# A sigmoid-attention and soft-MoE kernel: V products one unit behind their scores instead of two, two sigmoid buffers instead of three, 57 weight units loaded beside attention instead of 56

## The chip, the cores and the metric

One Trainium2 chip, one core of it. The metric is the device time of one execution in microseconds (us), as the median of several runs. Every engine has its own instruction queue, which it works through in order: PE (matmuls; PEld is its weight loads), DVE, ACT, POOL, and SP, which here only issues DMAs.

## The reference, cut to what matters

```python
# attention: batch 8, heads 12, sequence 448, head size 64, float32
scores = q @ k.T / sqrt(64) - log(448)
attn = 1 / (1 + exp(-scores))            # a sigmoid, no softmax
x = (attn @ v)                           # -> (8 * 448, 768)
# soft MoE: 8 experts, 4 slots each, inner size 1024
logits = x @ phi                         # (3584, 32)
d = softmax of logits over the 3584 rows
slots = d.T @ x                          # (32, 768)
slot_out[e] = relu(slots[e] @ w1[e]) @ w2[e]
out = (softmax of logits over the 32 slots) @ slot_out
```

## The kernel before, in words

**Attention.** The 96 heads go in 48 pairs (`NP`), of which one head lies on partitions 0 to 63 and the other on 64 to 127. Three units `(p, c)` with `c` 0 to 2 take 128 keys each of pair `p`, and a fourth, `c == NFK`, takes the last 64 keys of two pairs at once, so that two pairs make 7 units, a batch 21, and the whole 168 (list `seq`). A unit is: `score(u)`, four fp32 matmuls (eight passes on PE) of 64-by-64 weights and 448 columns, in the four quarters of the array, into a PSUM tile `sc` (L155 to L163); one sigmoid by ACT over 128 by 896 numbers into an SBUF tile `att` (L164, L165); `weigh(u)`, the four products of V with `att` into the PSUM tiles `av` (L168 to L190). There are two `sc` tiles and three `att` tiles.

**The order** is written by hand: one loop over steps `i` (L409) issues `score` of unit `i` and then `weigh` of unit `i - LAG`, with `LAG = 2`. All engines take their instructions in that order. The products of the last pair (three units) are issued at L177 on the whole height of the array, 128 by 64, instead of on quarters.

**Beside it.** When a pair's products are done, ACT copies one half out of PSUM (`evac_a`, L193) and DVE adds the other (`evac_b`, L197). DVE transposes x into `y` in small pieces (L212), so many us of them in a step as the table `rate` says (`PACE` where it says nothing). After each batch but the last, counted in steps from `u = (b + 1) * per_b + LAG`: `logits_job` in step u+1 (PE L230, DVE copies and maxima), `softmax_b` in step u+2 (two small sigmoids on ACT, L263 and L264), `softmax_c` in step u+3 (DVE L269 to L279), `slot_job` in step u+9 (PE L284, which needs all of `y` and what `softmax_c` made). The last batch is finished by `last_job`: logits (L230), softmax, slot inputs (L291, L295).

**The weights.** 128 units (64 of w1, 64 of w2) of 128 by 768 numbers, 384 KB each, pass through a ring of `N_A + N_B` = 70 SBUF tiles. `N_A` = 56 of them (`wa`) are there from the start and are filled beside attention, paced by L419. The other 14 (`wb`) lie in the memory that the attention tiles leave: their loads stand on SP behind the attention's loads (L465), in order, and each waits until the tiles that lay there were last used. The list `first` (L112) sets the order in memory: qk0, qk1, v0, vl, att0, qk2, x0, att1, att2, v1, x1, y. So the first `wb` tiles come free with the last scores, and the last three (`wb11` to `wb13`) only when `y` was last read, by the last slot matmuls (L291). From then on every load waits for a tile of the ring and goes out as w1 parts (L472), w2 steps (L579) and output tiles (L536, L537) free them; the output, 28 DMAs of 384 KB, ends the kernel.

Of the kernel before, what the change touches and what calls it, by code (L numbers as in the profile page):

```python
# [11 lines left out]
AF = mybir.ActivationFunctionType  # L12
# [5 lines left out]
DM, NSLOT, E, SPE, F = 768, 32, 8, 4, 1024  # L18
P = 128
NFK = 3  # L20
LAG = 2
PACE = 1.25
SLOT_AT = 9
W_STEPS = 140
# [2 lines left out]
NFC = F // P  # L27
HALF = DM // 2
UNIT = 768
N_A = 56  # L30
N_B = 14
QW = 2 * S
NP = B * NPR
WARM = 8
# [14 lines left out]
def soft_moe_attention(ctx: ExitStack, tc: tile.TileContext, qk, v, vl, phi, w1, w2, cst, out):  # L49
    nc = tc.nc  # L50
# [17 lines left out]
    def lt_of(b):  # L68
        return lts[b // 4][:, b % 4, :]
# [9 lines left out]
    def ring_tile(dt=F32):  # L79
        n = state["ring"]  # L80
        state["ring"] = n + 1
        n %= N_A + N_B
        if n < N_A:
            return wpa.tile([P, UNIT], dt, name=f"wa{n}")
        return state["wpb"].tile([P, UNIT], dt, name=f"wb{n - N_A}")

    def load_unit():
        n = state["next"]
        if n >= len(units):
            return  # L90
        state["next"] = n + 1
        u = units[n]
        t = ring_tile()[:]
        nc.sync.dma_start(t, w1[u[1:]] if u[0] == "w1" else w2[u[1:]])
        utile[u] = t
# [4 lines left out]
    with ExitStack() as actx:  # L100
# [8 lines left out]
        def hold(kind, n=""):  # L109
            return ap.tile(kinds[kind], F32, name=f"{kind}{n}")  # L110

        first = [("qk", 0), ("qk", 1), ("v", 0), ("vl", ""), ("att", 0), ("qk", 2), ("x", 0)]  # L112
        first += [("att", 1), ("att", 2), ("v", 1), ("x", 1)]
        held = {k: hold(*k) for k in first}
        xs = [held.pop(("x", t)) for t in range(2)]
        yt = ap.tile([P, 2, 4, TR, NBK, BLK], F32, name="y")
# [2 lines left out]
        def get(*k):  # L119
            return held.pop(k, None) or hold(*k)  # L120
# [16 lines left out]
        def load_qk(p):  # L137
            if p < NP:
                t = get("qk", p % 3)
                nc.sync.dma_start(t[:], qk[p])  # L140
                qkts[p] = t
# [13 lines left out]
        def score(u):  # L155
            p, c = u
            sc = ps_sc.tile([P, 2, 512], F32, name="sc")
            for t in range(2):
                pt, k0 = (p, c * P + t * 64) if c < NFK else (p + t, NFK * P)
                for h, r in enumerate(heads):  # L160
                    nc.tensor.matmul(  # L161
                        sc[64 * t:64 * t + 64, h, 0:S], qkts[pt][r, S + k0:S + k0 + 64], qkts[pt][r, 0:S],
                        start=True, stop=True)  # L163
            att = get("att", seq.index(u) % 3)  # L164
            nc.scalar.activation(att[:], sc[:, :, 0:S], AF.Sigmoid, bias=nbias[:], scale=QSCALE)  # L165
            atts[u] = att

# [40 lines left out]
        def turns(t, k0, n):  # L208
            def one(a, g):
                src = xs[t][32 * a:32 * a + 32, k0:k0 + n, :]  # L210
                src = bass.AP(src.tensor, src.offset + BLK * g, [src.ap[0], src.ap[1], [P, nblk(g)], [1, BLK]])
                nc.vector.transpose(ys[t][32 * g:32 * g + 32, a, k0:k0 + n, 0:nblk(g), :], src)  # L212

            for g in range(4):
                for a in range(4):
                    todo.append((0.0335 * n * nblk(g) + 0.18, lambda a=a, g=g: one(a, g)))
# [18 lines left out]
        def logits_job(b):  # L235
            lg = ps_sc.tile([P, 2, 512], F32, name="sc")[:, 0, :]
            logits(lg, b, range(NPR))
            nc.vector.tensor_copy(lt_of(b)[0:64, :], lg[0:64, 0:P])
            nc.vector.tensor_copy(lt_of(b)[64:128, 0:96], lg[64:128, 0:96])
            softmax_a(b)  # L240
# [16 lines left out]
            nc.vector.tensor_scalar(zt[:, 0:P], ls, new, None, op0=ALU.subtract)  # L257
            dts[b] = t1

        def softmax_b(b):  # L260
            zt, pe = dts[b][:, 0, :], dts[b][:, 1, :]
            n = P if b == 0 else P + 1
            nc.scalar.activation(pe[:, 0:n], zt[:, 0:n], AF.Sigmoid)  # L263
            nc.scalar.activation(zt[:, 0:n], zt[:, 0:n], AF.Sigmoid, scale=-1.0)  # L264

        def softmax_c(b):
            zt, pe = dts[b][:, 0, :], dts[b][:, 1, :]
            n = P if b == 0 else P + 1
            nc.vector.reciprocal(zt[:, 0:n], zt[:, 0:n])  # L269
            nc.vector.tensor_tensor(out=pe[:, 0:n], in0=pe[:, 0:n], in1=zt[:, 0:n], op=ALU.mult)  # L270
            nc.vector.transpose(zt[:, 0:P], pe[:, 0:P])
            if b == 0:
                nc.vector.tensor_reduce(out=mz[:, 2:3], in_=pe[:, 0:P], axis=AX.X, op=ALU.add)
            else:
                zb = small.tile([P, 1], F32, name="zb")
                nc.vector.tensor_reduce(out=zb[:], in_=pe[:, 0:P], axis=AX.X, op=ALU.add)
                nc.vector.scalar_tensor_tensor(
                    out=mz[:, 2:3], in0=mz[:, 2:3], scalar=pe[:, P:P + 1], in1=zb[:], op0=ALU.mult, op1=ALU.add)
            nc.vector.transpose(lt_of(b), lt_of(b))  # L279
# [19 lines left out]
        def slot_job(b):  # L299
            work(B * S)  # L300
            sl = ps_sc.tile([P, 2, 512], F32, name="sc")[:, 0, :]
            slot_mm(sl, dts[b][:, 0, 0:P])
            if b == 0:
                nc.vector.tensor_copy(acc[:], sl[:, 0:SLN])
            else:
                nc.vector.scalar_tensor_tensor(  # L306
                    out=acc[:], in0=acc[:], scalar=dts[b][:, 1, P:P + 1], in1=sl[:, 0:SLN],
                    op0=ALU.mult, op1=ALU.add)
# [71 lines left out]
        seq = []  # L380
# [4 lines left out]
        early, middle, late, rate = {}, {}, {}, {}  # L385
        for b in range(B):
            u = b * per_b + LAG
            late[u + 10] = [lambda: turns(0, 0, 3)]
# [3 lines left out]
        for b in range(B - 1):  # L392
            u = (b + 1) * per_b + LAG
            early[u + 1] = [lambda b=b: logits_job(b)]
            middle[u + 2] = [lambda b=b: softmax_b(b)]
            late[u + 3] = [lambda b=b: softmax_c(b)]
            late[u + SLOT_AT] = [lambda b=b: slot_job(b)]
            rate.update({u - 2: 1, u - 1: 1, u: 0, u + 1: 0, u + 2: 1.2, u + 3: 0.6, u + 4: 1.2})
        for i in range(u + 10, u + 31):
            rate[i] = PACE + 0.1  # L400
        todo = deque()
# [6 lines left out]

        for i in range(len(seq) + LAG):  # L409
            for f in early.get(i, ()):  # L410
                f()
            if i < len(seq):
                u = seq[i]
                score(u)
                if u[1] == NFK:
                    load_qk(u[0] + 3)
                elif u[0] % 2 == 1 and u[1] == NFK - 1:
                    load_qk(u[0] + 3)
                while state["next"] < min(N_A, (i + 1) * N_A // W_STEPS):  # L419
                    load_unit()  # L420
# [7 lines left out]
            for f in middle.get(i, ()):  # L428
                f()
            if i >= LAG:  # L430
                u = seq[i - LAG]
                weigh(u)
# [31 lines left out]

    for _ in range(N_B):  # L465
        load_unit()
# [184 lines left out]
```

## Time and profile before

| | before |
|---|---|
| median of 3 runs | 382.33 us (381.64 to 383.32) |
| the profiled execution, its own time | 382.41 us |
| its span, first instruction to last | 380.6 us |
| granted TensorE clock, mean of the span | 0.973 |
| PE busy | 357.8 us, 94% |
| ACT busy | 224.3 us, 59% |
| DVE busy | 252.7 us, 66% |
| DMA | 95.26 MB, mean 250 GB/s |

Read it by stages, not as one mean: until about 279 us PE works without a pause and the DMA queue has room; from about 285 us until the end the 16 DMA engines are busy without a pause, and PE waits now and then. Times in the views are us from the span's start. A matmul's end is modelled; a block of eight overlapping matmuls is listed with 0.93 us, though the next block starts 0.75 us after it.

### The profile page before, as it was taken

The page shows a single profiled execution, that of the slowest core. Times are in us where ns is not written, and L with a number is a line of the kernel's source. Part 1 is how long each engine was busy: PE and PEld are TensorE (multiplying, and loading weights), DVE is VectorE, ACT ScalarE, POOL GpSimd, SP SyncE. Part 2 cuts the span into 40 slices and gives each one's busy share as a digit, 9 for nine tenths or more (in the row PEclk, how much of TensorE's full clock was granted, in tenths as well). Part 3 has the DMA queues.
Part 4 walks back from the last instruction along what each step waited for, and adds up shares of the span by engine and source line. Part 5 has one row for each costly group of instructions (what it writes and reads, how often), then busy time and mean ns, then how long its engine had stood idle before and what let it go on. Part 6 is the DMA issues. An engine that isn't in the chain of part 4 may idle for free.

```text
span 380.6 us, 10176 instructions
## 1 busy us (share of the span) xinstructions
PE 357.8 (94%) x4132; PEld 158.4 (42%) x4132; DVE 252.7 (66%) x681; ACT 224.3 (59%) x310; POOL 4.9 (1%) x23
## 2 busy tenths in 40 slices
PE   8999999999999999999999999999999969989750
PEld 5444444444444444444444444444446533422430
DVE  0148868886889688788968896886846762132560
ACT  4777766766768677667767676776761213422450
POOL 0000000000000000000000000000000000100000
PEclk9999999999999999999999999999999987999895
DMA  7677575766656675757667575534369999999998
GB/s 258 212 252 255 165 257 176 254 217 189 219 190 216 235 241 197 236 180 246 213 186 250 169 236 203 146 102 134 91 219 388 397 397 400 397 400 395 396 399 301
DMA packets 42382, 95.26 MB, mean 250 GB/s; under 512 B 4448, under 2 KB 18528, under 8 KB 42336
## 3 DMA queue, kind: packets, MB, share of 16 engines
q1 hardware_dynamic: 42336, 94.62, 72.0%
q8 instruction: 32, 0.52, 0.5%
q14 instruction: 14, 0.11, 0.1%
HBM read 83.59 MB, written 11.01 MB: 249 GB/s over the span
## 4 chain that ended last, share of the span: by engine, by line
PE 83%; DVE 7%; DMA 3%; ACT 2%; issue 1%; DVEq 0%; ACTq 0%
PE sc L161 34%; PE av L190 33%; PE po L579 5%; PE sc L230 3%; PE sc L284 3%; DMA wb<-in_w_dram 2%; PE pt L517 2%; PE av L376 1%; PE ph L536 1%; DVE tmp L486 1%; DMA out_dram<-wa 1%; DVE tmp L485 1%; DVE wa L537 1%; PE pt L536 1%; PE av L177 1%
## 5 line engine op out<-in xcount | busy, mean ns | idle before, releaser
L165 ACT ACTIVATE att<-sc,nbias 128x896 f32<-128x896 f32 x168 | 169.2, 1008 | 85.2 <-PE sc L161 82.1
L161 PE MATMUL sc<-qk 64*64 64x448 f32 x1344 | 157.2, 538 | 0.4 <-ACT att L165 0.4
L212 DVE STREAM_TRANSPOSE y<-x 32x384 f32<-32x384 f32 (+5 forms) x352 | 143.4, 407 | 5.7
L190 PE MATMUL av<-att,v 64*64 64x448 f32 x1128 | 131.4, 536 | 0.0
L161 PEld LDWEIGHTS sc<-qk 64*64 64x64 f32 x1344 | 49.8, 133 | 72.6 <-issue 60.8
L190 PEld LDWEIGHTS av<-att,v 64*64 64x64 f32 x1128 | 43.1, 133 | 62.8 <-issue 61.3
L197 DVE TENSOR_TENSOR x<-x,av 128x448 f32<-128x448 f32 x47 | 29.2, 621 | 41.4 <-PE av L190 29.7
L579 PE MATMUL po<-wa,hw 128*32 128x384 f32 x224 | 24.8, 513 | 0.3 <-DMA wa<-in_w_dram 0.3
L193 ACT COPY x<-av 128x448 f32<-128x448 f32 x47 | 24.6, 523 | 0.0
L190 PE MATMUL av<-att,vl 64*64 64x448 f32 x192 | 22.4, 536 | 0.0
L472 PE MATMUL ph<-wa,phit 128*32 128x256 f32 x336 | 18.5, 379 | 0.0
L472 PEld LDWEIGHTS ph<-wa,phit 128*32 128x32 f32 x336 | 10.7, 110 | 6.9
L536 PE MATMUL ph<-lt,wb 128*128 128x384 f32 x28 | 12.7, 453 | 1.0 <-DVE lt L566 1.0
L537 DVE COPY wa<-pt 128x384 f32<-128x384 f32 x21 | 10.9, 554 | 2.9 <-PE pt L536 2.6
L537 ACT COPY wa<-ph 128x384 f32<-128x384 f32 x21 | 9.8, 480 | 4.9 <-PE ph L536 4.2
L230 PE MATMUL sc<-x,phit 128*32 128x96 f32 (+1 forms) x384 | 12.3, 262 | 0.3 <-DVE x L202 0.3
L230 PEld LDWEIGHTS sc<-x,phit 128*32 128x32 f32 x384 | 9.9, 110 | 6.2 <-ACT x L193 4.9
L536 PE MATMUL pt<-lt,wb 128*128 128x384 f32 x28 | 10.4, 373 | 1.6 <-DVE lt L566 1.6
L190 PEld LDWEIGHTS av<-att,vl 64*64 64x64 f32 x192 | 7.3, 133 | 10.7 <-issue 10.7
L306 DVE SCALAR_TENSOR_TENSOR acc<-acc,t,sc 128x192 f32<-128x192 f32 x6 | 2.5, 413 | 13.5 <-PE sc L284 13.5
L488 ACT COPY t<-tmp 128x32 f32<-128x32 f32 x8 | 1.7, 218 | 15.8 <-DVE tmp L486 15.8
L507 DVE CAST tmp<-lt 128x128 fp32r<-128x128 f32 x8 | 1.8, 227 | 13.7 <-PE pt L517 13.4
(106 smaller groups left out, 178.6 us busy)
## 6 DMA issues: line engine op xcount, KB each, us to landing
wa<-in_w_dram SPq DMA_DIRECT2D x112, 384.0 KB, 6.2
qk<-in_qk_dram SPq DMA_DIRECT2D x48, 448.0 KB, 3.5
v<-in_v_dram SPq DMA_DIRECT2D x48, 192.0 KB, 2.6
out_dram<-wa SPq DMA_DIRECT2D x21, 384.0 KB, 5.2
wb<-in_w_dram SPq DMA_DIRECT2D x16, 384.0 KB, 6.1
out_dram<-wb SPq DMA_DIRECT2D x7, 384.0 KB, 7.7
vl<-in_vl_dram SPq DMA_DIRECT2D x24, 64.0 KB, 2.6
csb<-in_cst_dram SPq DMA_DIRECT2D x1, 128.0 KB, 4.6
```

Of the source, the lines that this page charges most:

```text
L161: nc.tensor.matmul(sc[64 * t:64 * t + 64, h, 0:S], qkts[pt][r, S + k0:S + k0 + 64], qkts[pt][r, 0:S], start=True, stop=True)
L165: nc.scalar.activation(att[:], sc[:, :, 0:S], AF.Sigmoid, bias=nbias[:], scale=QSCALE)
L190: nc.tensor.matmul(o[t][r, 0:S], w, att[row, h, :], start=start, stop=stop)
L193: nc.scalar.copy(x_of(p), avs[p][1][:, 0:S])
L197: nc.vector.tensor_tensor(out=x_of(p), in0=x_of(p), in1=av[0][:, 0:S], op=ALU.add)
L212: nc.vector.transpose(ys[t][32 * g:32 * g + 32, a, k0:k0 + n, 0:nblk(g), :], src)
L230: nc.tensor.matmul(lg[32 * j:32 * j + 32, 0:BLK * nblk(j)], phi_sb[:, hp, :], blocks(x_of(b * NPR + hp), j, nblk(j)), start=(hp == 0), sto ...
L284: nc.tensor.matmul(sl[32 * a:32 * a + 32, 0:SLN], zt[:, c * BLK:(c + 1) * BLK], yt[:, :, a, :, c, :], start=(c == 0), stop=(c == NBK - 1))
L472: nc.tensor.matmul(ph[32 * j:32 * j + 32, 0:256], sT[:, kc, :], utile[("w1", e, j, kc // 3)][:, kc % 3 * 256:(kc % 3 + 1) * 256], start=(k ...
L536: nc.tensor.matmul(pf[:, 0:HALF], ct_of(m), st, start=True, stop=True)
L537: (nc.scalar.copy, nc.vector.tensor_copy)[n % 2](ov, pf[:, 0:HALF])
L579: nc.tensor.matmul(po[32 * fl:32 * fl + 32, 0:HALF], h[:, k:k + NSLOT], ut, start=(n == 0), stop=(n == 2 * E - 1))
```

## The change

`LAG` becomes 1: the order on PE is S(i), W(i-1), S(i+1), W(i) where it was S(i), W(i-2), S(i+1), W(i-1) (S for `score`, W for `weigh`). There are two `att` tiles instead of three, which leaves 3584 bytes of each partition; the ring gets 57 `wa` tiles and 13 `wb` tiles, and the list `first` another order. The two small sigmoids go to ACT one in step u+3 and one in step u+4 instead of both in step u+2, `softmax_c` to step u+5 instead of u+3, and the rates of the DVE transposes around them are shifted.

```diff
-LAG = 2
+LAG = 1
-N_A = 56
-N_B = 14
+N_A = 57
+N_B = 13
...
-        first = [("qk", 0), ("qk", 1), ("v", 0), ("vl", ""), ("att", 0), ("qk", 2), ("x", 0)]
-        first += [("att", 1), ("att", 2), ("v", 1), ("x", 1)]
+        first = [("qk", 0), ("qk", 1), ("v", 0), ("vl", ""), ("qk", 2), ("x", 0)]
+        first += [("att", 0), ("att", 1), ("v", 1), ("x", 1)]
...
-            att = get("att", seq.index(u) % 3)
+            att = get("att", seq.index(u) % 2)
...
-        def softmax_b(b):
+        def softmax_b(b, k):
...
-            nc.scalar.activation(pe[:, 0:n], zt[:, 0:n], AF.Sigmoid)
-            nc.scalar.activation(zt[:, 0:n], zt[:, 0:n], AF.Sigmoid, scale=-1.0)
+            if k == 0:
+                nc.scalar.activation(pe[:, 0:n], zt[:, 0:n], AF.Sigmoid)
+            else:
+                nc.scalar.activation(zt[:, 0:n], zt[:, 0:n], AF.Sigmoid, scale=-1.0)
...
-            middle[u + 2] = [lambda b=b: softmax_b(b)]
-            late[u + 3] = [lambda b=b: softmax_c(b)]
+            for k in range(2):
+                middle[u + 3 + k] = [lambda b=b, k=k: softmax_b(b, k)]
+            late[u + 5] = [lambda b=b: softmax_c(b)]
...
-            rate.update({u - 2: 1, u - 1: 1, u: 0, u + 1: 0, u + 2: 1.2, u + 3: 0.6, u + 4: 1.2})
+            rate.update({u - 2: 1, u - 1: 1, u: 0, u + 1: 0, u + 2: 1, u + 3: 1.2, u + 5: 0.6, u + 6: 1.2})
```

How that moves the instructions, at three places. The first is PE in the middle of attention, at the scores of unit 7 and what follows; the names in brackets are the semaphores for which a row waits (`Activation` counts ACT's instructions, `DMAHW` a landing). Before:

```order
L161 MATMUL sc_203<-qk2_90 64x448 [waits DMAHW7_49,Activation_49]
L161 MATMUL sc_203<-qk2_90 64x448 x3
L190 MATMUL av10_181<-att2_179,v1_94 64x448 x2
L190 MATMUL av11_182<-att2_179,v1_94 64x448 x2
L161 MATMUL sc_216<-qk2_90 64x448 [waits Activation_49]
L161 MATMUL sc_216<-qk2_90 64x448 x3
L190 MATMUL av10_181<-att0_195,v1_94 64x448 x2
L190 MATMUL av11_182<-att0_195,v1_94 64x448 x2
L161 MATMUL sc_231<-qk2_90 64x448 [waits Activation_49]
```

And the same scores now:

```order
L161 MATMUL sc_207<-qk2_89 64x448 [waits DMAHW7_49,PE_49]
L161 MATMUL sc_207<-qk2_89 64x448 x3
L190 MATMUL av10_174<-att0_199,v1_93 64x448 [waits Activation_49]
L190 MATMUL av10_174<-att0_199,v1_93 64x448
L190 MATMUL av11_175<-att0_199,v1_93 64x448 x2
L161 MATMUL sc_224<-qk2_89 64x448 [waits PE_49]
L161 MATMUL sc_224<-qk2_89 64x448 x3
L190 MATMUL av00_231<-att1_212,v0_162 64x448 [waits DMAHW2_49,DVE_49,Activation_49]
```

The wait for ACT has moved from the first matmul of a score (which needed the sigmoid of two units earlier, to have its `sc` tile back) to the first matmul of a product (which needs the sigmoid of its own unit); a score now waits only for PE's own matmuls of two units earlier.

The second place is PE at the end of attention: the last scores, the products of the last pair (L177, on another shape of the array), and the logits of the last batch (L230). Before:

```order
L161 MATMUL sc<-qk_3142 64x448 x4
L190 MATMUL av_3252<-att_3266,vl 64x448 x2
L190 MATMUL av_3293<-att_3266,vl 64x448 x2
L161 MATMUL sc<-qk_3142 64x448 x4
L177 MATMUL av_3293<-att_3278,v_3238 64x448 x2
L230 MATMUL sc<-x_91,phit 32x96 x2
...
L230 MATMUL sc<-x_95,phit 32x128 x2
L177 MATMUL av_3293<-att_3290,v_3238 64x448 x2
L177 MATMUL av_3293<-att_3304,v_3238 64x448 x2
```

And now:

```order
L161 MATMUL sc<-qk_3148 64x448 x4
L177 MATMUL av_3288<-att_3285,v_3233 64x448 x2
L161 MATMUL sc<-qk_3148 64x448 x4
L177 MATMUL av_3288<-att_3299,v_3233 64x448 x2
L230 MATMUL sc<-x_90,phit 32x96 x2
...
L230 MATMUL sc<-x_94,phit 32x128 x2
L177 MATMUL av_3288<-att_3308,v_3233 64x448 x2
```

The same matmuls stand there, but one product of the last pair now lies between the last two scores and one, not two, behind the logits: PE changes the shape five times instead of three.

The third place is SP behind attention, where the loads into the memory of the attention tiles stand. Before:

```order
L94 DMA wb2_3459<-in_w1_dram 128x768 [waits DMAHW7_49,DMAHW0_49,PE_49]
L94 DMA wb3_3461<-in_w1_dram 128x768 [waits PE_49,Activation_49]
L94 DMA wb4_3463<-in_w1_dram 128x768 [waits DMAHW6_49]
L94 DMA wb5_3465<-in_w1_dram 128x768 [waits DVE_49,PE_49]
L94 DMA wb6_3467<-in_w1_dram 128x768
L94 DMA wb7_3469<-in_w1_dram 128x768 [waits DMAHW1_49,PE_49,Activation_49]
L94 DMA wb8_3471<-in_w2_dram 128x768 [waits DMAHW2_49,PE_49,Activation_49]
L94 DMA wb9_3473<-in_w2_dram 128x768 [waits DMAHW3_49,DVE_49,PE_49]
L94 DMA wb10_3475<-in_w2_dram 128x768 [waits DMAHW4_49]
L94 DMA wb11_3477<-in_w2_dram 128x768 [waits DVE_49,PE_49,DMAHW5_49,Activation_49,Pool_49]
```

And now:

```order
L94 DMA wb2_3461<-in_w1_dram 128x768 [waits DMAHW1_49,DMAHW0_49,PE_49]
L94 DMA wb3_3463<-in_w1_dram 128x768 [waits DMAHW7_49,PE_49]
L94 DMA wb4_3465<-in_w1_dram 128x768 [waits DVE_49,PE_49]
L94 DMA wb5_3467<-in_w1_dram 128x768 [waits Activation_49]
L94 DMA wb6_3469<-in_w1_dram 128x768
L94 DMA wb7_3471<-in_w2_dram 128x768 [waits DMAHW2_49,PE_49,Activation_49]
L94 DMA wb8_3473<-in_w2_dram 128x768 [waits DMAHW3_49,DVE_49,PE_49]
L94 DMA wb9_3475<-in_w2_dram 128x768 [waits DMAHW4_49]
L94 DMA wb10_3477<-in_w2_dram 128x768 [waits DVE_49,PE_49,DMAHW5_49,Activation_49,Pool_49]
```

The row that waits for five semaphores, for the release of `y`, is `wb11` before and `wb10` now. Counted from 0 over all 128 units it is unit 67 both times (56 + 11 and 57 + 10). The wait for x0 (`DVE_49,PE_49`, released by the logits of the last batch) has come forward from `wb5` to `wb4`.

## The prediction

> **What bounds the kernel now.** I read the page, then the busy times by stage.
>
> ```profile
> span 380.6 us, 10176 instructions
> ...
> 4.83:279.25 274.42, 274.04 (x3229) 115.80 (x3229) 208.81 (x545) 191.61 (x229) 0.00 (x0) 1.00 0.63 203
> 279.25:287.34 8.09, 7.33 (x157) 5.32 (x159) 3.16 (x14) 4.28 (x12) 0.00 (x0) 1.00 0.92 310
> 287.34:352.68 65.34, 60.56 (x702) 26.41 (x691) 29.29 (x97) 17.13 (x47) 3.99 (x18) 0.95 1.03 396
> 352.68:380.60 27.92, 12.11 (x44) 7.36 (x44) 10.89 (x21) 9.78 (x21) 0.00 (x0) 0.75 0.96 365
> ```
>
> After the stage come its length and the busy times of PE, PEld, DVE, ACT and POOL; at the end the granted clock, the DMA share and GB/s. Attention (first row) is PE alone: 274.04 of 274.42 us, at full clock, DMA at 203 GB/s. From 287.34 us on the DMA engines are full, at 396 GB/s. So a change in attention counts if it moves PE, and behind attention only if it moves bytes or the moment from which they flow without a pause.
>
> Does anything make PE wait in attention? The groups:
>
> ```profile
> L165 ACT ACTIVATE att<-sc,nbias 128x896 f32<-128x896 f32 x168 | 169.2, 1008 | 85.2 <-PE sc L161 82.1
> L161 PE MATMUL sc<-qk 64*64 64x448 f32 x1344 | 157.2, 538 | 0.4 <-ACT att L165 0.4
> L161 PEld LDWEIGHTS sc<-qk 64*64 64x64 f32 x1344 | 49.8, 133 | 72.6 <-issue 60.8
> ```
>
> PE waited for a sigmoid 0.4 us in all, and a sigmoid takes 1.008 us. With the products two units behind, that is no wonder: between a score and its product PE has four other blocks of work (a product, a score, a product, a score). The change leaves two. So the question is how much of that cover a sigmoid uses, and I went to the timeline of a plain unit (start, length, engine):
>
> ```profile
> 139.88 0.93 PE L161 MATMUL sc<-qk 64*64 64x448 f32 x8
> ...
> 140.63 0.93 PE L190 MATMUL av<-att,v 64*64 64x448 f32 x8
> ...
> 140.94 1.01 ACT L165 ACTIVATE att<-sc,nbias 128x896 f32<-128x896 f32 x1 [0.50 <-PE sc L161]
> ...
> 141.39 0.93 PE L161 MATMUL sc<-qk 64*64 64x448 f32 x8
> ...
> 141.76 0.15 PEld L190 LDWEIGHTS av<-att,v 64*64 64x64 f32 x4 [0.22 <-issue]
> ...
> 142.14 0.56 PE L190 MATMUL av<-att,v 64*64 64x448 f32 x4
> ```
>
> A block starts every 0.75 us (139.88, 140.63, 141.39, 142.14), a unit takes 1.50. The score that starts at 139.88 has its sigmoid from 140.94 to 141.95. In the new order its product takes the block at 142.14. That is 0.19 us after the sigmoid's end, and the weights of that block, loaded at 141.76 now, can't be loaded so early, since the whole matmul, its weight load too, stands behind the wait.
>
> **The change part by part: the lag.** What does it cost PE when a sigmoid releases it? The trace shows it once, at the third score, which waits for the first sigmoid:
>
> ```profile
> 5.88 1.91 ACT L165 ACTIVATE att<-sc,nbias 128x896 f32<-128x896 f32 x2 [3.65 <-PE sc L161]
> 6.94 0.21 PEld L161 LDWEIGHTS sc<-qk 64*64 64x64 f32 x8 [1.15 <-ACT att L165]
> 6.94 0.98 PE L161 MATMUL sc<-qk 64*64 64x448 f32 x8 [0.38 <-ACT att L165]
> ...
> 7.74 0.93 PE L190 MATMUL av<-att,v 64*64 64x448 f32 x8
> ```
>
> The first of the two sigmoids ends at 5.88 + 1.008 = 6.89; the load starts at 6.94, so the release takes 0.05 us. The next block starts 0.80 us later instead of 0.75, so the weight load in the open costs 0.05. For the plain unit: 141.95 + 0.05 + 0.05 = 142.05, against 142.14. **Spare: 0.09 us; the wait costs nothing.** The other end: weight loads that stand in the open between blocks of different shape cost more, by the chain of waits:
>
> ```profile
> 144.57 1.45 PE sc L230 x42
> 146.02 0.91 PE sc L161 x8
> 147.68 0.75 PE sc L161 x8
> ```
>
> 0.91 - 0.75 = 0.16 us. With that, 141.95 + 0.05 + 0.16 = 142.16, which is 0.02 late. A score starts 0.75 us after the product before it, and that product hangs on the sigmoid of a score two places back, so one lateness is paid once in two units: 84 x 0.02 = 1.7 us. I take 0, because the row that shows this very wait is the nearer one; 1.7 is the upper end. A gain is excluded, since the blocks follow each other without a gap already.
>
> A load's own recorded duration is 133 ns (the third row of the groups). Even if all of it stood in the open, the product would start at 141.95 + 0.05 + 0.13 = 142.13, still in time.
>
> The longer lag had another use, to cover a late sigmoid. ACT's queue is late in one place of each batch:
>
> ```profile
> 148.56 1.01 ACT L165 ACTIVATE att<-sc,nbias 128x896 f32<-128x896 f32 x1 [0.47 <-PE sc L161]
> ...
> 149.47 0.30 ACT L263 ACTIVATE t<-t 128x129 f32<-128x129 f32 x1
> ...
> 149.80 0.32 ACT L264 ACTIVATE t<-t 128x129 f32<-128x129 f32 x1
> ...
> 150.02 0.52 ACT L193 COPY x<-av 128x448 f32<-128x448 f32 x1
> ...
> 150.43 2.08 ACT L165 ACTIVATE att<-sc,nbias 128x896 f32<-128x896 f32 x2
> ```
>
> Sigmoids follow each other by 1.50 us, so the next was due at 148.56 + 1.50 = 150.06, and started at 150.43, 0.37 late, behind two small sigmoids and a copy. With the new lag this would have cost 0.37 - 0.09 = 0.28 us, seven times: 2.0 us. That is what the split prevents. A small sigmoid starts 0.91 us after a big one and holds ACT for 0.33 (149.47 to 149.80): 148.56 + 0.91 + 0.33 = 149.80, before 150.06. Steps u+3 and u+4 have no copy (the third and seventh unit of seven bring one). A copy alone fits too: 0.91 + 0.53 = 1.44, under 1.50. The small sigmoid's input is ready in step u+2 already, where it runs now. Nothing late is left on ACT, so this costs and brings 0.
>
> `softmax_c` on DVE starts two units later. Its reader is the slot job; DVE's pieces that must precede that end earlier:
>
> ```profile
> 157.50 1.47 DVE L212 STREAM_TRANSPOSE y<-x 32x96 f32<-32x96 f32 x5
> ...
> 159.64 1.51 PE L284 MATMUL sc<-y,t 128*32 128x192 f32 x32
> ```
>
> 158.97 against 159.64, 0.67 us spare. DVE does the same work without a hole in another order, and transposes fill the time until the second small sigmoid: 0. If that cover went, a hole of up to 2 x 1.50 = 3.0 us less 0.67 would be paid at each slot job.
>
> SP's V loads hang on the products, which come one block earlier against the scores; they land in 2.6 us (the page's part 6) and are used four units, 6 us, later. The 57th weight load is 0.39 MB in 274 us at 203 of 396 GB/s: no cost. Beginning of the kernel: the third score or the first product waits for the same sigmoid, 0.
>
> **The end of attention** has two more changes of array shape.
>
> ```profile
> 277.49 0.93 PE L161 MATMUL sc<-qk 64*64 64x448 f32 x8
> ...
> 278.35 0.97 PE L177 MATMUL av<-att,v 128*64 128x448 f32 x4
> ```
>
> 278.35 - 277.49 - 0.75 = 0.11 for one, and 0.16 for the score after logits above: 0.27, so **+0.3 us** on everything that waits for the last product.
>
> **The 57th unit.** Behind attention DMA is the limit, so a unit loaded earlier is worth 393,216 bytes / 396 GB/s = 0.99 us, if the queue doesn't run dry. It could: the loads stand in order and unit 67 waits for `y` in both kernels, with 11 `wb` loads ahead of it before and 10 now. The waits of SP's queue between 268 and 289 us, the issues at its release, and the landings (us, minimum, median, maximum) of the first two `wb` loads and of the last three:
>
> ```profile
> SPq L94 <- PE av L291: 2.0, 1, 2.0
> ...
> 287.54 1.28 SPq L94 DMA_DIRECT2D wb<-in_w_dram  x3
> ...
> L94 SPq DMA_DIRECT2D wb<-in_w_dram x2: 328/379/430, 272.1 to 273.9; - x2
> ...
> DMA to landing us min/median/max: 3.0/3.1/3.2
> ...
> L94 SPq DMA_DIRECT2D wb<-in_w_dram x3: 328/423/430, 287.5 to 288.4; - x3
> ...
> DMA to landing us min/median/max: 5.0/5.6/6.1
> ```
>
> With an empty queue a load lands in 3.0 us; unit 67 took 5.0, so 2.0 us of work stood ahead of it. One unit less leaves 1.0: the queue doesn't run dry, and the full 0.99 counts. Against it stands the 0.3 us above, and that `wb4` to `wb7` are released later than their neighbours (for x0 the logits, now behind one more product). The 1.0 us left would hide the 0.3; since I can't show that the late releases leave it whole, I charge the 0.3.
>
> Sum: 382.4 (profiled execution; median 382.33) - 0.99 + 0.3 + 0 = **381.7 us**.
>
> **The rivals.** *No gain from the 57th unit*: the later release of x0 eats the last 1.0 us of queue, and the gate of unit 67 sets the end in both: 382.4, with the end of attention 382.7. For it: the gate has not moved. Against: 2.0 us of queue.
>
> *Slower, products with an open weight load*: the weights of a product whose wait ended late are not loaded under the score that is still streaming but behind it. Then each product pays the 0.05 us of the third score, 165 x 0.05 = 8.3, that is 390.7 us (at 0.16 even 26 us). It decides as soon as a sigmoid ends after the point of early load, which is 141.76 in the plain unit, and it ends at 141.95 there. For it: no row shows a late release while PE is streaming. Against: the loads at 141.76 run under a score that uses the same rows of the array and cost its block nothing.
>
> A rule of the Trainium skill would make this rival the forecast. "TensorE: Matmul & The Clock Gate", section "The mechanism" (packing of small matmuls), says that weight loads overlap running matmuls only where their row groups differ; by it the time would be 390.7 us, by the row at 141.76 it is 381.7. The row differs from the rule, and I go by the row.
>
> *Faster*: between 279 and 285 us DMA is not full.
>
> ```profile
> 279.00:285.00 6.00, 5.72 (x76) 3.64 (x74) 1.59 (x8) 3.50 (x9) 0.00 (x0) 1.00 0.86 274
> ```
>
> At 396 GB/s 6 x (1 - 274/396) = 1.85 us could be had there. If the releases that come earlier (the products of unit 164, which free `wb2`, end one block sooner) fill it, this comes on top of 0.99 less 0.3: 382.4 - 0.7 - 1.85 = 379.9. Against: most of the releases there have not moved forward.
>
> **How the numbers follow.** Forecast 0.60, no gain 0.20, slower 0.13, faster 0.07. A measurement of this kernel tells about 0.5%, 1.9 us, from no change: forecast and no gain lie within it (0.80), the others outside. The three runs spread from 381.64 to 383.32, 0.7 below and 1.0 above their median. Forecast less 0.7 is 381.0, no gain plus 1.0 is 383.7. The lower end goes 0.5 further, for a hole between 279 and 285 us that is filled in part. So 380.5 to 383.7 holds the forecast and no gain, 0.80, and the 1.7 us of the wait's upper bound (381.7 + 1.7 = 383.4).
>
> **What would show it.** Right: a plain unit still takes 1.50 us, with the product's weight load about 0.05 us behind its sigmoid's end and not 0.38 ahead of the block; the slot jobs start when they did; unit 67 lands about 4 us after its issue; attention ends 0.3 us later and the span 0.7 us earlier. Wrong: units of 1.55 us, big sigmoids that start late behind something else on ACT, a slot job that waits for DVE, or a DMA share under 1 between 287 and 291 us.

## The result, and the profile after

| | before | after |
|---|---|---|
| median | 382.39 us (381.22 to 383.44, 20 runs) | 383.47 us (381.89 to 385.47, 20 runs) |
| the profiled execution, its own time | 382.41 us | 383.62 us |
| its span | 380.6 us | 381.8 us |

The changed kernel takes 1.0029 of the time before, 95% interval 1.0018 to 1.0040: 0.7 to 1.5 us slower. A second comparison, on another chip (e13 below), gave 1.0017 (1.0002 to 1.0031), and both hold a loss of 0.7 to 1.2 us. The time lies inside the range of the forecast only because the range was drawn wide enough for the rival without a gain; the direction was wrong: 0.7 us less was forecast, and about 1 us more came.

Attention first. The groups of the profile after (busy time and mean of one, then the idle time before them and what ended it):

```profile
L165 ACT ACTIVATE att<-sc,nbias 128x896 f32<-128x896 f32 x168 | 169.1, 1007 | 86.8 <-PE sc L161 84.3
L161 PE MATMUL sc<-qk 64*64 64x448 f32 x1344 | 157.2, 539 | 0.0
L190 PE MATMUL av<-att,v 64*64 64x448 f32 x1128 | 131.4, 536 | 0.4 <-ACT att L165 0.4
L190 PEld LDWEIGHTS av<-att,v 64*64 64x64 f32 x1128 | 41.2, 131 | 65.4 <-ACT att L165 61.5
```

The weight loads (PEld) of the products now wait for sigmoids, 61.5 us in all, but the products themselves only 0.4 us, at the first one. Two plain units in the timeline after:

```profile
132.81 1.01 ACT L165 ACTIVATE att<-sc,nbias 128x896 f32<-128x896 f32 x1
...
133.26 0.93 PE L161 MATMUL sc<-qk 64*64 64x448 f32 x8
...
133.87 0.29 PEld L190 LDWEIGHTS av<-att,v 64*64 64x64 f32 x8 [0.46 <-ACT att L165]
134.01 0.93 PE L190 MATMUL av<-att,v 64*64 64x448 f32 x8
...
134.76 0.93 PE L161 MATMUL sc<-qk 64*64 64x448 f32 x8
...
135.51 0.93 PE L190 MATMUL av<-att,v 64*64 64x448 f32 x8
```

The sigmoid ends at 132.81 + 1.01 = 133.82, the load starts at 133.87, the block at 134.01, and the next product 1.50 us later. The wait is there and costs nothing.

The end of attention in the timeline after, then in that before:

```profile
276.99 0.93 PE L161 MATMUL sc<-qk 64*64 64x448 f32 x8
277.85 0.97 PE L177 MATMUL av<-att,v 128*64 128x448 f32 x4
278.76 0.98 PE L161 MATMUL sc<-qk 64*64 64x448 f32 x8
279.67 0.97 PE L177 MATMUL av<-att,v 128*64 128x448 f32 x4
280.57 1.30 PE L230 MATMUL sc<-x,phit 128*32 128x96 f32 x40
281.80 0.97 PE L177 MATMUL av<-att,v 128*64 128x448 f32 x4
282.70 0.55 PE L221 MATMUL av<-csb,x 128*128 128x128 f32 x3
```

```profile
275.98 0.93 PE L161 MATMUL sc<-qk 64*64 64x448 f32 x8
276.73 0.93 PE L190 MATMUL av<-att,vl 64*64 64x448 f32 x8
...
280.48 1.72 PE L177 MATMUL av<-att,v 128*64 128x448 f32 x8
282.13 0.66 PE L221 MATMUL av<-csb,x 128*128 128x128 f32 x4
```

The first transposes of x (L221) start at 282.70 instead of 282.13, 0.57 us later: 0.31 from the shape changes (from the last score but one to the first transposes 5.71 us, before 6.15 with one block of 0.75 us more in between), 0.19 from six slot products, each of which holds PE for 1.47 us now (before 1.44), and 0.08 from the start.

Then the DMA engines. Busy times by stage (the last two columns are the DMA share and GB/s), before and after:

```profile
276.00:284.00 8.00, 7.72 (x97) 3.60 (x90) 2.58 (x9) 5.57 (x10) 0.00 (x0) 1.00 0.62 201
284.00:288.00 4.00, 3.52 (x106) 3.07 (x108) 2.78 (x15) 1.40 (x6) 0.40 (x2) 1.00 1.00 369
288.00:292.00 4.00, 4.00 (x74) 2.36 (x70) 2.71 (x13) 0.31 (x1) 0.21 (x1) 1.00 1.04 389
292.00:300.00 8.00, 8.00 (x156) 4.79 (x151) 6.39 (x24) 1.58 (x6) 0.42 (x2) 1.00 1.02 391
```

```profile
276.00:284.00 8.00, 7.72 (x97) 2.97 (x89) 1.70 (x6) 5.95 (x10) 0.00 (x0) 1.00 0.67 191
284.00:288.00 4.00, 3.52 (x102) 3.33 (x102) 2.77 (x13) 1.54 (x7) 0.00 (x0) 1.00 1.02 374
288.00:292.00 4.00, 4.00 (x75) 2.31 (x70) 2.59 (x13) 0.31 (x1) 0.61 (x2) 1.00 0.98 334
292.00:300.00 8.00, 8.00 (x152) 4.81 (x148) 6.39 (x24) 1.58 (x6) 0.42 (x2) 1.00 1.00 383
```

The queue is full from 288 us on before (1.04, 389 GB/s); after, it isn't (0.98, 334). In a second profile of the changed kernel (e13 below) the rate of this stage is 371 GB/s, between the two, at a share of 1.07: the rate tells more than the share. From 276 to 300 us the changed kernel moves 8 x 10 - 4 x 5 + 4 x 55 + 8 x 8 = 344 KB less, 0.87 us at 396 GB/s. That is nearly the whole 57th unit (393 KB), which had come before 276 us.

### The profile page after: what moved, and what is told of

Read it like the earlier page. It is cut to its first block, busy times and chain, and to the rows that moved or that the text cites. A ratio compares the mean times of both kernels' runs of the same rounds, so it can differ in the third digit from the quotient of the medians.

```text
span 381.8 us, 10246 instructions
## 1 busy us (share of the span) xinstructions
PE 358.0 (94%) x4132; PEld 155.9 (41%) x4132; DVE 253.9 (66%) x681; ACT 223.7 (59%) x310; POOL 4.9 (1%) x23
## 4 chain that ended last, share of the span: by engine, by line
PE 76%; DMA 11%; DVE 6%; ACT 2%; issue 1%; DVEq 0%; SPq 0%; ACTq 0%
PE sc L161 34%; PE av L190 33%; DMA wa<-in_w_dram 8%; PE sc L230 3%; PE sc L286 3%; DMA wb<-in_w_dram 2%; PE av L378 1%; DMA out_dram<-wa 1%; DVE tmp L489 1%; DVE tmp L488 1%; PE av L177 1%; ACT lt L500 1%; DVE lt L499 1%; DVE cz L502 1%; DVE lt L505 1%
## 5 line engine op out<-in xcount | busy, mean ns | idle before, releaser
L190 PEld LDWEIGHTS av<-att,v 64*64 64x64 f32 x1128 | 41.2, 131 | 65.4 <-ACT att L165 61.5
L582 PE MATMUL po<-wa,hw 128*32 128x384 f32 x228 | 27.9, 494 | 0.4 <-DMA wa<-in_w_dram 0.3
L475 PE MATMUL ph<-wa,phit 128*32 128x256 f32 x342 | 19.8, 379 | 0.0
L539 PE MATMUL ph<-lt,wb 128*128 128x384 f32 x28 | 11.8, 421 | 1.1 <-DVE lt L569 1.0
L230 PE MATMUL sc<-x,phit 128*32 128x96 f32 (+1 forms) x384 | 12.3, 262 | 0.3 <-DVE x L202 0.3
L230 PEld LDWEIGHTS sc<-x,phit 128*32 128x32 f32 x384 | 9.9, 110 | 6.2 <-PE sc L161 4.9
L582 PEld LDWEIGHTS po<-wa,hw 128*32 128x32 f32 x228 | 6.6, 108 | 12.9 <-DMA wa<-in_w_dram 5.5
L539 PE MATMUL pt<-lt,wb 128*128 128x384 f32 x28 | 9.5, 341 | 1.6 <-DVE lt L569 1.6
L286 PE MATMUL sc<-y,t 128*32 128x192 f32 x224 | 10.7, 329 | 0.0
```

The lines of the kernel that those rows point to most:

```text
L190: nc.tensor.matmul(o[t][r, 0:S], w, att[row, h, :], start=start, stop=stop)
L230: nc.tensor.matmul(lg[32 * j:32 * j + 32, 0:BLK * nblk(j)], phi_sb[:, hp, :], blocks(x_of(b * NPR + hp), j, nblk(j)), start=(hp == 0), sto ...
L286: nc.tensor.matmul(sl[32 * a:32 * a + 32, 0:SLN], zt[:, c * BLK:(c + 1) * BLK], yt[:, :, a, :, c, :], start=(c == 0), stop=(c == NBK - 1))
L475: nc.tensor.matmul(ph[32 * j:32 * j + 32, 0:256], sT[:, kc, :], utile[("w1", e, j, kc // 3)][:, kc % 3 * 256:(kc % 3 + 1) * 256], start=(k ...
L539: nc.tensor.matmul(pf[:, 0:HALF], ct_of(m), st, start=True, stop=True)
L582: nc.tensor.matmul(po[32 * fl:32 * fl + 32, 0:HALF], h[:, k:k + NSLOT], ut, start=(n == 0), stop=(n == 2 * E - 1))
```

## The experiments

Two theories at first. One puts the loss into attention: the lag of one makes it longer, and the buffers that it leaves come late. The other puts it behind attention, into the 57th unit and the order of the buffers.

**e1_lag1_56**: the changed kernel with the ring of before.

```diff
-N_A = 57
-N_B = 13
+N_A = 56
+N_B = 14
```

> The changed kernel with 56 units beside attention and 14 behind it, as before; lag, sigmoid buffers and split stay changed. Theory A (the late end): attention ends 0.57 us later (in the trace of the changed kernel the first transposes on PE start at 282.70 us instead of 282.13), this alone makes the loss and the 57th unit brings nothing or a little: 383.4 to 384.2 us, at or above the changed kernel. Theory B (the short queue): the loss comes from the 57th unit, which leaves fewer loads queued when unit 67 is released, so that the DMA engines run short between 289 and 294 us; with 14 loads behind attention the queue covers the late end again: 382.3 to 382.7 us, as before the change.

Measured: 1.0032 (1.0017 to 1.0047), as the first theory has it. It is no clean test: with two sigmoid buffers the memory lies differently, and it is unit 66, not 67, that waits for `y`.

**e2_lag2_57**: the changed kernel with the old lag; 57 units, two buffers and the split stay.

```diff
-LAG = 1
+LAG = 2
```

> The changed kernel with the products two units behind their scores, as before; two sigmoid buffers, split and 57 units stay. Each sigmoid then waits for the product two units back to release its buffer, which ends 0.13 us after the sigmoid could have started by the trace's plain unit; no wait on PE expected, attention ends where it ended before (282.1 us) give or take 0.2. Theory A: no loss, and the 57th unit's 0.99 us in part: 381.5 to 382.4 us. Theory B: the queue is short here too: 382.9 to 383.5 us.

Measured: 0.9996 (0.9977 to 1.0015). Without the lag there is no loss. The 57th unit with its full 0.99 us should have given 0.9974, just outside this interval; with what the split costs (told below) the kernel gained 0.2 us.

**e3_old_tail**: the changed kernel with the last two products issued together, so three shape changes as before.

```diff
-            if i >= LAG:
+            if i >= LAG and i != len(seq) - 2:
                 u = seq[i - LAG]
+                if i == len(seq) - 1:
+                    weigh(seq[i - LAG - 1])
```

> The changed kernel with the products of the last pair put together again, three changes of array shape at the end instead of five (the last two scores stand together). Attention ends about 0.3 us earlier than in the changed kernel. Theory A: 383.2 us, 0.3 less than the changed kernel's 383.5. Theory B: within 0.2 us of the changed kernel, since the queue is as short.

Measured: 1.0025 (1.0007 to 1.0043). With the old tail there is still a loss; the 0.3 us of the tail itself are too small to be read from this interval.

**e4_before_late**: the kernel before with 0.55 us of extra matmuls ahead of the last transposes.

```diff
+                        warm(pw, 2)
                         turn_pe(px[0], p - 1)
```

> The kernel before with two idle matmuls (four passes, about 0.55 us by the ones already there: six passes take 0.83 us) put on PE behind the last product, so that attention ends as late as in the changed kernel, with 56 units. Theory A: slower by 0.5 to 1.1 us: 382.9 to 383.5 us. Theory B: the 2.0 us of loads that stand ahead of unit 67 hide it: 382.3 to 382.6 us.

Measured: 0.9995 (0.9980 to 1.0010), as the second theory has it. But in its trace the first load that waits for `y` goes out only 0.43 us later (287.97 us), 0.14 us when a start that was 0.29 us slower is set aside: other work hid most of the delay. It doesn't show that a late release is free.

**e5_att_new** and **e6_att_old**: attention alone, of the changed kernel and of that before; everything from the weight ring's second part on is left out and the slot inputs are written out instead.

```diff
+    nc.sync.dma_start(out[0:P, 0:NKC * NSLOT].rearrange("p (k s) -> p k s", k=NKC), sT[:])
```

> Attention of the changed kernel by itself: everything behind the last slot inputs is left out (no loads behind attention, no experts, no combination; one small DMA of the slot inputs ends it). Read beside the same cut of the kernel before. Theory A (the lag costs in attention itself, more than one profile shows): 0.8 to 1.3 us more than the cut of the kernel before. Theory B (what the traces show is all: 0.3 us for two more changes of array shape, 0.03 us at each of six slot jobs): 0.4 to 0.6 us more, and the rest of the 1.1 us loss arises behind attention.

> Attention of the kernel before by itself, cut at the same place (no loads behind attention, no experts, no combination). About 288 us by the trace of the kernel before, where the last slot inputs are there at 287.9 us, with some 4 us for the DMA and the end: 290 to 293 us. It is the measure for the cut of the changed kernel.

Measured: 293.88 us (292.74 to 293.93) and 292.77 us (292.24 to 293.25), in ratios to the whole kernel 0.7663 (0.7650 to 0.7676) and 0.7642 (0.7630 to 0.7654). So attention is 0.8 to 1.1 us longer. The two profiled executions lie 1.6 us apart: 0.48 us arise between the eleventh score and the first transposes, with the block by which the lag moves that score set aside (the tail and the slot products again), 1.1 us at the start. The start is told in the last section; it varies from run to run in both kernels, so 0.5 us is what the change itself costs in attention.

**e7_unsplit**: the changed kernel with both small sigmoids in step u+2, as before.

```diff
-            for k in range(2):
-                middle[u + 3 + k] = [lambda b=b, k=k: softmax_b(b, k)]
-            late[u + 5] = [lambda b=b: softmax_c(b)]
+            middle[u + 2] = [lambda b=b: [softmax_b(b, k) for k in range(2)]]
+            late[u + 3] = [lambda b=b: softmax_c(b)]
```

> The changed kernel with both small sigmoids, the softmax behind them and the transposes' rates where they were before the change (step u+2, u+3), so that the split alone is undone. By the working of the prediction a big sigmoid then starts 0.37 us late once a batch, the product one unit behind waits 0.28 us for it, seven times 2.0 us: about 2.0 us more than the changed kernel, 385.4 us. The rival that PE has more cover than the plain unit shows: no more than 0.5 us over the changed kernel.

Measured: 1.0058 (1.0046 to 1.0071), 1.1 to 1.6 us above the changed kernel by its two comparisons. Its timeline shows the late sigmoid that the prediction priced:

```profile
44.61 0.30 ACT L264 ACTIVATE t<-t 128x128 f32<-128x128 f32 x1
44.94 0.31 ACT L266 ACTIVATE t<-t 128x128 f32<-128x128 f32 x1
45.15 0.52 ACT L193 COPY x<-av 128x448 f32<-128x448 f32 x1
45.57 2.06 ACT L165 ACTIVATE att<-sc,nbias 128x896 f32<-128x896 f32 x2
```

```profile
45.62 0.93 PE L161 MATMUL sc<-qk 64*64 64x448 f32 x8
46.63 0.98 PE L190 MATMUL av<-att,v 64*64 64x448 f32 x8
47.43 0.93 PE L161 MATMUL sc<-qk 64*64 64x448 f32 x8
```

The product starts 1.01 us after the score instead of 0.75, and the next block 0.80 after it: 0.31 us, seven times 2.2 us of attention. The forecast said 0.28 and 2.0.

**e8_lag_only**: the kernel before with the lag of one and the split, but 56 units and three buffers.

```diff
-LAG = 2
+LAG = 1
...
-            middle[u + 2] = [lambda b=b: softmax_b(b)]
-            late[u + 3] = [lambda b=b: softmax_c(b)]
+            for k in range(2):
+                middle[u + 3 + k] = [lambda b=b, k=k: softmax_b(b, k)]
+            late[u + 5] = [lambda b=b: softmax_c(b)]
```

> The kernel before with the lag of one unit and the split of the small sigmoids, but with three sigmoid buffers, 56 and 14 units and the old order in memory, so that 11 loads stand ahead of the release of y again and the loads wait for the same tiles as before. Theory A (the lag costs in attention or by itself): 383.4 to 384.2 us. Theory B (the late end of attention hurts only where fewer or later loads stand ahead of that release): hidden, 382.4 to 383.0 us.

Measured: 1.0019 (1.0005 to 1.0033), 0.2 to 1.3 us of loss without the 57th unit, between the two forecasts. It doesn't set the lag apart from a late end of attention: with the start set aside the first transposes come 0.7 us later than before, nearly as late as in e11 below, which lost 0.5 us.

The next four move attention's end by a known dose, in both directions and both kernels.

**e9_lag2_late** and **e11_before_late** (in `score`), **e10_lag1_early** and **e12_before_early** (in `weigh`):

```diff
-            for t in range(2):
+            for t in (0, 1) * (2 if u == seq[127] else 1):
```

```diff
-            for t in range(2):
+            for t in range(0 if u == seq[127] else 2):
```

> The changed kernel with a lag of two units and, on top, the scores of unit 127 issued twice (a plain block of scores takes 0.75 us on TensorE, so everything behind it, the releases of the last attention buffers too, comes 0.75 us later). Releases theory (with 57 units the loads at the end of attention wait for buffers, so each us by which the releases move goes into the end): 0.9996 of the kernel with the lag of two, plus 0.75 / 383 = 0.0020, so 1.0016, near the changed kernel. Lag theory (a late end of attention is hidden behind loads in hand, and the lag of one costs by something else): 0.9996 to 1.0000.

> The kernel before with the scores of unit 127 issued twice, 0.75 us more of TensorE well ahead of the end of attention, so that all the releases there move, not the last one alone. Releases theory without cover: 1.0020. Releases theory with the cover that the prediction claimed for 56 units (about 0.5 us of loads to spare at the gated load): 1.0007. Lag theory: 1.0000.

> The changed kernel without the eight matmuls of the V product of unit 127 (its sigmoids are not weighed, so this part of the output's sum is left out; 0.75 us of TensorE less, about 60 us before the end of attention). Releases theory: 1.0029 less 0.0020, so 1.0009. Lag theory: unchanged, 1.0025 to 1.0030.

> The kernel before without the eight matmuls of the V product of unit 127 (this part of the output's sum is left out; 0.75 us of TensorE less). If the releases bound the kernel before as well: 0.9980. If the loads in hand bound it (the transfer queue is full from 284 us on): 1.0000. Between the two, with part of the 0.75 us kept: about 0.9990.

Measured: e9 1.0020 (1.0002 to 1.0038), so 0.9 us over the same kernel without the delay; e11 1.0014 (0.9999 to 1.0029), 0.5 of the 0.75 us; e12 0.9997 (0.9982 to 1.0011): the kernel before gains nothing that can be measured from an earlier end. So it seems to stand at a corner, where later costs and earlier doesn't pay; the interval of e11 just includes no cost, so this is not shown. e10 gave 0.9999 (0.9985 to 1.0014), below both of its forecasts, but it failed as a dose. In its trace attention got only 0.1 us shorter. At the place of the product that is left out, two scores follow each other:

```profile
214.75 1.82 PE L161 MATMUL sc<-qk 64*64 64x448 f32 x16
216.92 0.98 PE L190 MATMUL av<-att,v 64*64 64x448 f32 x8 [0.35 <-ACT att L165]
```

PE is through with them 0.75 us early, and then the next product waits for the sigmoid of its own unit, as the lag of one makes it. The 0.1 us is about the spare that the prediction worked out for a unit (0.09). So this kernel says nothing of the dose. But it has the lag of one, ends attention nearly as late as the changed kernel, and yet took 0.7 to 1.1 us less than that: either two kernels of like traces differ by so much in their ratios, or the lag of one doesn't cost by itself.

The last four ran side by side on one chip.

**e13_after_again** is the changed kernel, **e15_lag2_57_again** is e2, **e16_old_tail_again** is e3. **e14_after_half_slot** leaves out half of one slot product, where no sigmoid is waited for:

```diff
-        def slot_mm(sl, zt):
-            for c in range(NBK):
+        def slot_mm(sl, zt, n=NBK):
+            for c in range(n):
...
-            slot_mm(sl, dts[b][:, 0, 0:P])
+            slot_mm(sl, dts[b][:, 0, 0:P], NBK // 2 if b == 5 else NBK)
```

> The changed kernel unchanged, on one chip with the three below. If its loss is the kernel's own: 1.0029 again, within 1.0018 to 1.0040. If ratios differ from chip to chip or call to call: anywhere from 0.9999 to 1.0030.

> The changed kernel with half of the slot product of the sixth batch left out (eight of its sixteen matmuls with their part of the sum, 0.73 us of TensorE, behind a product, where no sigmoid is waited for). Releases theory: the attention buffers come 0.73 us earlier and the end with them, 0.0019 under the changed kernel of the same call. Lag theory (something of the lag that is not the time of the releases): as the changed kernel.

> The changed kernel with a lag of two units, as e2. Releases theory: the last buffers come 0.35 us earlier than with the lag of one (0.25 instead of 0.6 us behind those of before, starts aside), so 0.0009 under the changed kernel of the same call. If the lag costs by something else as well: 0.0020 to 0.0033 under it, as in the first call.

> The changed kernel with the last two products issued together as before (three array-shape changes less work at the end: 0.31 us), as e3. Releases theory: 0.0008 under the changed kernel of the same call, level with the kernel with the lag of two. If the lag of one costs by something else: as the changed kernel, or within 0.0004 of it.

Measured: e13 1.0017 (1.0002 to 1.0031), e14 0.9994 (0.9982 to 1.0006), e15 0.9993 (0.9983 to 1.0003), e16 1.0014 (1.0001 to 1.0026). Half a slot product less, 0.73 us, brings back 0.9 us: in the changed kernel the end of attention seems to count in full. The old lag brings back the same. The old tail, which moves the end of attention by 0.31 us, brings 0.1 us. By the intervals each of these differences is good to about 0.6 to 0.7 us, so the first two are clear of nothing and the third isn't. The runs with the lag of two took 382.58 us in the median, none over 383.0; those of the changed kernel 383.35.

The time goes with how much the DMA queue has moved when it is full for good. From the packets of each trace I summed the bytes moved until 300 us, with the difference of the starts set aside, and give the difference to the kernel before in us at 396.5 GB/s:

| kernel | us ahead (+) at 300 us | time against before, us |
|---|---|---|
| e14 half slot product | +0.75 | -0.2 |
| e12 before, early | +0.70 | -0.1 |
| e15, e2 lag of two, 57 units | +0.43, +0.18 | -0.3, -0.2 |
| e10 | +0.24 | 0.0 |
| e4 before, late end | +0.17 | -0.2 |
| e13 and the first trace of the changed kernel | 0.0, -0.21 | +0.7, +1.1 |
| e16, e3 old tail | -0.25, -0.45 | +0.5, +1.0 |
| e9 lag of two, late | -0.29 | +0.8 |
| e11 before, late | -0.56 | +0.5 |
| e8 lag alone | -0.77 | +0.7 |
| e1 | -1.46 | +1.2 |
| e7 unsplit | -1.99 | +2.2 |

Where a row has two numbers, the first belongs to the run named first; in the row of e13 the second is the first comparison of the changed kernel. Over the fifteen traces a us behind costs about 0.85 us, and the correlation is -0.9, or -0.8 without the last two rows. A row sets one profiled execution beside the time of many, and the changed kernel fits worst: it lies up to 0.6 us above this line.

## Why the prediction was wrong, step by step

**The wait of the products, 0: right.** The row at 133.87 shows the load 0.05 us behind the sigmoid's end, and units of 1.50 us. So the slower rival, 390.7 us, fell. The rule that the prediction took from the Trainium skill, "TensorE: Matmul & The Clock Gate", section "The mechanism", would have made it the forecast; the trace disagrees with that rule: the first four loads of a block run from 133.87 to 134.02 while the score that started at 133.26 still streams, on the same rows of the array, and the product starts on time at 134.01. The same section also lets a load go ahead that is for the background weight buffer; that half, which the prediction left out, the trace doesn't contradict.

**The small sigmoids, 2.0 us if not split: right**, with 2.2 us of attention in the trace of e7. Only 1.1 to 1.6 of them reached the time.

**The end of attention, +0.3: right in the tail (0.31), short by 0.19.** "The slot jobs start when they did" held against the scores, but six of the seven hold PE 0.03 us longer, with the old lag as well (e15, five of seven), with the layout of before as well (e8, six), and not in e7 (1.44, all seven). So it comes with the split, the later `softmax_c` and the shifted rates, which e7 takes back together, not with the lag.

**The 57th unit, -0.99: wrong, and this is the step that failed.** The forecast read that unit 67 landed 5.0 us after its issue, 3.0 with an empty queue, and concluded that 2.0 us of work stood ahead of it, of which 1.0 would be left: "the queue doesn't run dry". After, the same row reads:

```profile
L94 SPq DMA_DIRECT2D wb<-in_w_dram x3: 328/423/430, 288.1 to 289.0; - x3
...
DMA to landing us min/median/max: 4.3/4.9/5.4
```

Unit 67 went out at 288.10 us (before 287.54) and landed 4.3 us later, just about what was forecast. But a landing is that of the slowest of 16 DMA engines: each load raises its semaphore 16 times, and the traces have the time of each part. Before, the ninth of 16 parts of unit 67 was there at 291.00 us, 3.5 us after the issue, and the last at 292.54: the 2.0 us were for the most part the lag of the slowest engines. With an empty queue the ninth part takes 2.7 to 2.9 us (units 57 and 58 before), so that only 0.6 to 0.8 us of work stood ahead of the middle engines, less than the one unit that was taken away. After, the ninth part was there at 291.13, 3.0 us after the issue, and in the second profile (e13) 2.7 us after it: a queue that is empty or nearly so. The middle engines had run dry, as the 334 and 371 GB/s between 288 and 292 us show, against 389 before. The forecast had named a DMA share under 1 between 287 and 291 us as its sign of being wrong; it reads 0.99 in the one profile and 1.03 in the other, too coarse a sign. Unit 66 did land 1.0 us earlier (290.52 instead of 291.56); unit 67 landed 0.17 earlier. So the rival *no gain from the 57th unit* was the nearer one: the moment at which unit 67 goes out sets the end. e2 and e15 show it without the lag: 0.2 and 0.3 us came in place of 0.99, with the longer slot products in them.

There is a plain reason for it. The memory of the 57th `wa` tile is that of the third sigmoid buffer, which served as `wb` tiles from 279 to 285 us on anyway. By their number the loads from unit 60 on go out no earlier: unit 60 at 279.80 us (before 279.79), 61 at 281.48 (280.44), 64 at 282.86 (282.46), 66 at 285.49 (284.92). Only four units moved forward, 56 from 272.1 to 234.5 us and 57 to 59 by 2.2 to 2.8 us, and between 276 and 284 us the queue had room for them before (share 0.62).

**The lag itself, 0 in the sum: right for PE, but not for the time, and the cause stays open.** In place of -0.99 + 0.3 the four runs on one chip give, step by step, -0.3 us for all that the changed kernel has but the lag and the longer tail (e15), +0.8 for the lag with the old tail (e16 against e15; 0.2 to 1.4 by the intervals), and +0.1 for the tail: 0.6 us in all. The end of attention comes at the same time in e15 and e16, so it isn't what makes the 0.8. e3 against e2 gives 1.1 us in the same way. e10, with the lag of one and no loss, speaks against a cost of the lag itself.

Of the 0.8 us, 0.7 are there at 300 us as bytes that were not moved. The stage from 288 to 292 us, in e16 and then in e15:

```profile
288.00:292.00 4.00, 4.00 (x74) 2.37 (x70) 2.72 (x13) 0.31 (x1) 0.61 (x2) 1.00 0.90 293
```

```profile
288.00:292.00 4.00, 4.00 (x75) 2.33 (x70) 2.67 (x13) 0.31 (x1) 0.61 (x2) 1.00 1.01 364
```

The first of the loads that wait for `y` goes out at the same time in both (287.98 and 288.02 us). But SP is held up behind it, as the longest of these three issues shows (the numbers are the shortest, the median and the longest in ns), again in e16 and then in e15:

```profile
L94 SPq DMA_DIRECT2D wb<-in_w_dram x3: 328/425/1531, 288.0 to 288.8; - x3
```

```profile
L94 SPq DMA_DIRECT2D wb<-in_w_dram x3: 328/424/430, 288.0 to 288.9; - x3
```

In e16 SP needs 1.53 us for unit 69, so that unit 70 goes out at 290.45 instead of 289.40 us. In e15 the next issue is the long one, that of unit 70 (1.35 us). The last section tells what goes with this: a 16 KB packet of the instruction queue. It begins 0.9 to 1.1 us behind the issue of unit 67 in both profiles of the changed kernel, in e3, e16 and e9 (where attention also ends 0.9 us late), which lost 0.5 to 1.1 us, and 1.3 us or more behind it in the kernel before, e4, e10, e12, e14 and e15, which lost nothing. e2 doesn't fit (0.7 us, and no loss). e7, e8 and e11 lost at 1.5 to 1.8 us, but there attention ends 0.7 us late or more, and in e1 it is another unit that waits for `y`. No run moved this packet, so that it makes the loss is a guess; the guess would cover e10, which a cost of the lag itself doesn't.

In the profiled execution after, the stage from 340 to 360 us moves 384 GB/s, against 394 before, which is 200 KB or 0.5 us. In the second profile (e13) it is 396, so this part belongs to one execution and not to the change.

**Charging the late end, since "I can't show that the late releases leave it whole"**: the doubt was right, but a charge of 0.3 beside a gain of 0.99 that wasn't there could not give the right sign.

## What to carry to other kernels

A landing time is that of the slowest DMA engine; to see how much work stands ahead of a load, take the middle of its 16 parts, or look at the GB/s stage by stage. A buffer that is moved from one stage's use to another's need not bring what its bytes take in a full queue: if the later loads, by their number, wait for the same releases as before, it brings only what is left of its lead when they go out. And where a full queue follows a stage, look how much work is in hand there before a change uses it up: with less in hand, a delay of the stage, or of the queue that issues the loads, can turn into time.

## What the runs showed of the hardware

**The start.** The matmuls that run ahead of attention are twice as slow until a moment that varies from run to run, and the granted clock in the rows of the profile reads 1.00 all the while. The timelines of e2 and of e8, which issue the same instructions until the second score:

```profile
3.20 1.34 PE L378 MATMUL av<-acc 128*128 128x128 f32 x7
4.47 1.73 PE L161 MATMUL sc<-qk 64*64 64x448 f32 x16
```

```profile
3.20 1.70 PE L378 MATMUL av<-acc 128*128 128x128 f32 x7
4.83 2.54 PE L161 MATMUL sc<-qk 64*64 64x448 f32 x16
```

In e2 the passes change from 0.213 to 0.11 us apart at about 3.9 us, in e8 not before 6.3 us; over all the traces this makes 1.2 us between the earliest and the latest start, alike for both lags (0.6 us in the mean). It is a part of the spread of single runs, and a loss of 0.5 us can't be read from the span of one execution without setting it aside. The Trainium skill, "TensorE: Matmul & The Clock Gate", Part 1, tells of such a half-rate clock until a free-running window of 3.4 us has been busy; the traces agree in the half rate and in a moment that varies, and no run here shows the window itself.

**A late weight load is free while a matmul streams**, even 0.14 us ahead of its own block (133.87 to 134.01), and costs 0.05 us where nothing streams (46.63 in e7, next block 0.80 us later).

**SP's issues stand still beside the instruction queue.** In all sixteen traces with the weights behind attention a 16 KB packet of the instruction queue (q8 on the page) runs for 0.9 to 1.1 us soon after the loads that wait for `y` have begun to go out, and one issue of SP lasts until 0.36 to 0.37 us after its end: in e16 the packet runs from 288.96 to 289.98 us and the issue of unit 69 from 288.82 to 290.36, in e15 the packet ends at 290.38 and the issue of unit 70 at 290.75. Such an issue takes 0.8 to 1.5 us instead of the usual 0.33 to 0.43. Why SP is held isn't shown.
